# Attention on TensorE: every matmul and transpose issued in source order

## The chip, the cores and the metric

The kernel runs on one core of a Trainium2 chip. The metric is the device time of one execution in microseconds; the number to be predicted is the median of the runs of the changed kernel.

## The reference, cut to what matters

Attention with a position bias, followed by two feed-forward layers. The change is in the attention.

```python
B, H, S, D = 4, 8, 576, 64
scores = q @ k.T / sqrt(D) + bias          # bias: a small network of relative positions, per head
attn = exp(scores - scores.max(-1)) / sum   # row softmax
x = attn @ v                                # then two feed-forward layers on 2304 x 512
```

## The kernel before

Attention is done for 16 units. A unit n is one pair of heads of one batch entry. It has nine steps s: steps 0 to 7 are a block of 128 queries of one head against all 576 keys, and step 8 is the last 64 queries of both heads. A step goes through these stages:

- `scores` (L374): matmuls of the queries with the keys into a PSUM tile `s` (two buffers). Each product is made in two parts, high and low, and two halves of the keys, so a step of 128 queries is four instructions of 288 columns; step 8 has ten.
- VectorE (L378) adds the bias, writes `u` and reduces the row extreme into `stat`; ScalarE (L394) takes the exponential and writes the probabilities `p` (`pm` for step 8) and their row sums.
- `trans` (L432, L437 for step 8): a group of four transposes of 128 x 128 into a PSUM tile `tr`, which one copy moves to `ptm` in SBUF (L424 on VectorE or L422 on ScalarE, by the string PT_EVAC).
- `trans_rem` (L443, and L445 with c = 3): the keys beyond 512, one or two transposes into a tile `tr` of their own, copied to `ptr`.
- `invert` and `turn_inv` (L411): reciprocals of the row sums, spread out and turned by three or two transposes into a tile `tr`, copied to `inv`. The tile of three is copied by ScalarE; the tile of two by VectorE and then a short ScalarE copy.
- `av` (L458, L462): the product with the values into a PSUM tile `av`, and `av_out` (L471), which multiplies by `inv`.

The tiles named `tr`, from `trans`, `trans_rem` and `turn_inv` alike, share three PSUM buffers. A new tile can start only when the copy out of the buffer that it takes has ended.

`slot_of_two(i)` writes out the work of a slot: the scores of its two steps, the AV of older steps (`AV` gives the slots), their exponentials, the reciprocals, the turn of `inv`, and the transposes of the two steps of the slot before. Nine slots, a period, hold two units. Steps of the loading of the feed-forward weights (`load.one_step`, L243 to L255) and a part of the next unit's preparation (`prep`, L346 to L349) are woven in on the other engines.

The source order is not the order of issue. When the program is built, a scheduler lays out a fixed order for every engine by its own plan of the times: an instruction whose inputs or buffer are not ready in the plan lets later ones of its engine pass. On the chip each engine then works through its list in that order. `with tc.issue_after(x)` binds the instructions made inside to come behind x on the same engine. Before, there is one such edge in this part, which keeps the transposes of a slot behind the last score of the slot:

```python
            with tc.issue_after(last_s[0].ins):
                trans(t)
```

Of the kernel before, what the change touches and what calls it, by code (L numbers as in the profile page):

```python
# [1 line left out]

# [1 line left out]

# [14 lines left out]
P = 128  # L19
B, H, S, D = 4, 8, 576, 64  # L20
# [4 lines left out]
HS = S // 2  # L25
# [71 lines left out]
def block_kernel(ctx: ExitStack, tc: tile.TileContext, q, k, v, mlp, w_in, w_out, w_gate, w_val, w_out2, dist_d,  # L97
                 rows_d, out):
    nc = tc.nc
# [199 lines left out]
    Pm = [apool.tile([P, S], F32, name=f"pm{i}") for i in range(2)]  # L299
    ident = apool.tile([P, P], F32, name="ident")  # L300
    stat = apool.tile([P, 5, NSTEP, 2], F32, name="stat")
    low, sums = [stat[:, i, :, 0] for i in range(2)], [stat[:, i, :, 0] for i in range(2, 5)]
    spread = apool.tile([P, 5 * P], F32, name="spread")
# [10 lines left out]
    def load_v(n):  # L314
        vn[n] = a2.tile([P, 10, D], F32, name="vn")
        return nc.sync.dma_start(vn[n], v[n])

    def load_bias(p, c):
        n = min(P, S - P * c)
        rows_of = nbias[c][15 : 15 + n * (8 * RK - 1)].rearrange("(i q) -> i q", i=n)  # L320
        for h in range(2):
            o = bias_t[c][:, h] if c < 4 else bias_m[64 * h : 64 * h + 64]
            i = rows_of[:, RK * (2 * p + h) : RK * (2 * p + h) + S]
            if c == 4 and h == 1:
                nc.sync.dma_start(o[:, 0:512], i[:, 64:S])
                nc.sync.dma_start(o[:, 512:S], i[:, 0:64])
            else:
                nc.sync.dma_start(o, i)
# [23 lines left out]
    NS = NU * NSTEP  # L352
    ptm = apool.tile([P, 2, 4, S], F32, name="ptm")
    ptr = apool.tile([P, S], F32, name="ptr")
    pts, us, avs, last_u, last_s = {}, {}, {}, [None], [None]

    seq = [(n, s) for n in range(NU) for s in range(NSTEP)]

    def keys(s, h, a):

        if s < 8 or h == 0:
            return [(HS * a, 0, HS)]
        return [(64, 0, HS)] if a == 0 else [(64 + HS, 0, HS - 64), (0, HS - 64, 64)]

    def scores(t):
        n, s = seq[t]
        Q, K = Qs[n % 2], Ks[n % 2]
        ps = pp.tile([P, 2, 512], F32, name="s")
        todo = [(s % 2, s // 2)] if s < 8 else [(0, 4), (1, 4)]
        for a in range(2):  # L370
            mm = [(h, c, r, part) for h, c in todo for r in range(2) for part in keys(s, h, a)]
            for i, (h, c, r, (k0, o, w)) in enumerate(mm):
                q0 = (0, S + P)[h] + P * c if c < 4 else (512, S)[h]
                last_s[0] = nc.tensor.matmul(ps[:, a, o : o + w], Q[:, q0 : q0 + P], K[:, r, h, k0 : k0 + w],  # L374
                                             start=(i == 0), stop=(i == len(mm) - 1))
        u = a2.tile([P, S], F32, name="u", bufs=3)
        bt = bias_t[s // 2][:, s % 2] if s < 8 else bias_m
        last_u[0] = nc.vector.tensor_tensor_reduce(  # L378
            out=halves(u), in0=ps[:, :, 0:HS], in1=halves(bt), op0=ALU.add, op1=ALU.min, scale=-0.125, scalar=3e38,
            accum_out=low[n % 2][:, s : s + 1])  # L380
        us[t] = u
# [10 lines left out]
    def expo(t):  # L392
        n, s = seq[t]
        nc.scalar.activation(probs(t), us.pop(t), AF.Exp, bias=low[n % 2][:, s : s + 1], scale=-1.0,  # L394
                             accum_out=sums[n % 3][:, s : s + 1])
# [11 lines left out]
    def turn_inv(n, c0, c1):  # L407

        ps = pp.tile([P, 4, P], F32, name="tr", bufs=3)
        for c in range(c0, c1):  # L410
            nc.tensor.transpose(ps[:, c % 3], spread[:, P * c : P * c + P], ident)  # L411
        if c1 == 3:
            evac("A", inv[:, 0 : 3 * P].rearrange("p (c q) -> p c q", c=3), ps[:, 0:3])
        else:
            evac("V", inv[:, 3 * P : 4 * P], ps[:, 0])
            for h in range(2):
                r = slice(64 * h, 64 * h + 64)
                evac("VA"[h], inv[r, 4 * P : S], ps[r, 1, r])

    def evac(eng, dst, src):  # L420
        if eng == "A":
            nc.scalar.copy(dst, src)  # L422
        else:
            nc.vector.tensor_copy(dst, src)  # L424

    def trans(t):
        n, s = seq[t]
        if s < 8:
            ps = pp.tile([P, 4, P], F32, name="tr", bufs=3)
            c, h = divmod(s, 2)  # L430
            for kc in range(4):
                nc.tensor.transpose(ps[:, kc], pts[n, c][:, h, 64 * h + P * kc : 64 * h + P * kc + P], ident)  # L432
            evac(PT_EVAC[s], ptm[:, h, :, P * c : P * c + P], ps)
        else:
            ps = pp.tile([P, 4, P], F32, name="tr", bufs=3)
            for kc in range(4):
                nc.tensor.transpose(ps[:, kc], Pm[n % 2][:, P * kc : P * kc + P], ident)  # L437
            evac("VA"[n % 2], ptm[:, :, :, 512:S], ps.rearrange("p c (h q) -> p h c q", h=2))

    def trans_rem(n, c):  # L440

        ps = pp.tile([P, 4, P], F32, name="tr", bufs=3)
        nc.tensor.transpose(ps[:, 0], pts[n, c].rearrange("p h s -> p (h s)")[:, 512 : 512 + P], ident)  # L443
        if c == 3:
            nc.tensor.transpose(ps[0:64, 1], Pm[n % 2][:, 512:S], ident)  # L445
            for h in range(2):
                evac("AV"[h], ptr[64 * h : 64 * h + 64, 512:S], ps[0:64, 1, 64 * h : 64 * h + 64])
        evac("A", ptr[:, P * c : P * c + P], ps[:, 0])

    def av(n, a, g):  # L450
        if g == 0:
            avs[a] = pp.tile([P, 512], F32, name="av", bufs=1)
        ps = avs[a]
        vt = vn[n]
        cols = slice(HS * a, HS * a + HS)
        if g < 4:
            for h in range(2):
                nc.tensor.matmul(ps[64 * h : 64 * h + 64, 0:HS], vt[:, 4 * h + g], ptm[:, h, g, cols],  # L458
                                 start=(g == 0), stop=False)
        else:  # L460
            for h in range(2):
                nc.tensor.matmul(ps[64 * h : 64 * h + 64, 0:HS], vt[:, 8 + h], ptr[:, cols], start=False, stop=True)  # L462

    def av_out(n, a):
        p, b = divmod(n, B)
        i = S * b + HS * a
        while i < S * b + HS * a + HS:
            j, o = divmod(i, 2 * TW)
            w = min(2 * TW - o, S * b + HS * a + HS - i)
            k = i - S * b - HS * a  # L470
            nc.vector.tensor_tensor(out=xj[j][:, p, o : o + w], in0=avs[a][:, k : k + w],  # L471
                                    in1=inv[:, HS * a + k : HS * a + k + w], op=ALU.mult)
            i += w

    REM = {1: 0, 3: 1, 5: 2, 8: 3}
# [4 lines left out]
    for n in range(NU):  # L480
        i = (NSTEP * n + 5) // 2 + 2
# [5 lines left out]
    def steps(i):  # L487
        return [t for t in (2 * i, 2 * i + 1) if 0 <= t < NS]

    def slot_of_two(i):  # L490

        for t in steps(i):
            scores(t)
            n, s = seq[t]
            p, b = divmod(n, B)
            if s == 0:
                last_v[0] = load_v(n)
            if b == B - 1 and p + 1 < NPAIR and (s % 2 == 1 or s == 8):
                load_bias(p + 1, s // 2)
        for n, a, g in AV.get(i, ()):  # L500
            av(n, a, g)
            if g == 4:
                av_out(n, a)
        for t in steps(i):
            expo(t)
        for t in steps(i - 1):
            n, s = seq[t]
            if s in (5, 8):
                invert(n, s // 6 * 3, s // 6 * 2 + 3)
        for t in steps(i - 2):  # L510
            n, s = seq[t]
            if s in (5, 8):
                turn_inv(n, s // 6 * 3, s // 6 * 2 + 3)
        for t in steps(i - 1):
            n, s = seq[t]
            with tc.issue_after(last_s[0].ins):
                trans(t)
                if s in REM:
                    trans_rem(n, REM[s])
        for t in steps(i):  # L520
            if t in PREP:
                n, h = PREP[t]
                prep(n, h)
            for k, (n, h) in PREP.items():
                if h == 1 and n + 1 < NU and t == k + 3:
                    load_qk(n + 1)
# [6 lines left out]
    with ExitStack():  # L533
# [15 lines left out]
        ps = bp.tile([P, 2, 512], F32, name="s")[:, 0]  # L549
# [39 lines left out]
        for G in range(NG):  # L589
# [9 lines left out]
            ps = bp.tile([P, 2, 512], F32, name="s")  # L599
            for d0, d1 in ((0, min(nd, 512)), (512, nd)):  # L600
                for ct in range(4):
                    if d0 < d1:
                        nc.tensor.matmul(line(ps)[32 * ct : 32 * ct + 32, d0:d1], w2bd, hid[ct][:, d0:d1],
                                         start=True, stop=True)
# [44 lines left out]
        for i in range(NSLOT):  # L649
            slot_of_two(i)  # L650
            if i == NS // 2:
                w = keep.tile([P, 8 * TW], F32R, name="early")
# [119 lines left out]
        for part2, t in todo:  # L772
            for f in range(NH * part2, NH * part2 + NH):
# [3 lines left out]
                g = begun.pop(f) if f in begun and t == 0 else None  # L777
                if g is None:
                    g = hardswish(fp.tile([P, TW], F32, name="g", bufs=2), project(t, slots[2 * f % NALL]))
# [113 lines left out]
        for v, (p, j) in enumerate(visits):  # L893
# [9 lines left out]
            for n in range(2):  # L903
                t = 2 * j + n
# [48 lines left out]
```

## Time and profile before

| | |
|---|---|
| median of three runs | 1155.64 us (1153.95 to 1157.52) |
| the profiled execution: its time, its span | 1153.65 us, 1151.9 us |
| TensorE busy | 1129.9 us, 98% |
| VectorE busy | 770.0 us, 67% |
| ScalarE busy | 589.0 us, 51% |
| mean granted clock | 1.000 |

The bias is made from 0 to about 57 us, attention runs from there to about 341 us, and the two feed-forward layers fill the rest. PE is TensorE, PEld its weight loads, DVE VectorE, ACT ScalarE. The shares of the whole span average over stages with different limits, so attention is read from stretches of its own.

### The profile page before, as it was taken

The numbers are of one execution on the slowest core, as the hardware profiler recorded it, in microseconds if no ns is written. First come the engines' busy times: TensorE is split into PE (matmuls) and PEld (weight loads), VectorE is DVE, ScalarE is ACT, GpSimd is POOL, SyncE is SP. The second block draws the span as 40 slices with busy tenths as digits, with TensorE's granted clock in tenths as the row PEclk, the third lists the DMA queues.
The fourth block names the chain that finished last, engine by engine and source line by source line (L and its number), as shares of the span: only waits on it lengthen the run. The fifth ranks groups of instructions, "written<-read, shape, count | busy, mean of one in ns | idle before, by whom it ended". The sixth has DMA issues, their size and how long they took to land.

```text
span 1151.9 us, 19179 instructions
## 1 busy us (share of the span) xinstructions
PE 1129.9 (98%) x6878; PEld 1008.9 (88%) x6878; DVE 770.0 (67%) x1487; ACT 589.0 (51%) x1288; POOL 426.2 (37%) x340
## 2 busy tenths in 40 slices
PE   8799999999999999999999999999999999999998
PEld 3287777777789999999999999989899899998997
DVE  8987888897768888365376775585367656643443
ACT  7988888887765544454455454342333232221221
POOL 0154645554225432331347444261333223311311
PEclk9999999999999999999999999999999999999999
DMA  6854546364013665259467659976878848757532
GB/s 206 298 163 121 158 130 177 113 201 116 14 42 110 206 237 187 116 181 340 150 227 276 244 193 366 388 264 251 303 254 311 312 167 316 275 190 247 192 110 74
DMA packets 83503, 236.82 MB, mean 206 GB/s; under 512 B 9936, under 2 KB 12624, under 8 KB 83408
## 3 DMA queue, kind: packets, MB, share of 16 engines
q1 hardware_dynamic: 83408, 235.60, 59.4%
q8 instruction: 54, 0.88, 0.3%
q14 instruction: 41, 0.34, 0.1%
HBM read 154.15 MB, written 81.41 MB: 205 GB/s over the span
## 4 chain that ended last, share of the span: by engine, by line
PE 85%; DVE 5%; ACT 3%; issue 2%; POOL 1%; DMA 1%; DVEq 0%; ACTq 0%; POOLq 0%; SPq 0%
PE o L700 17%; PE h L834 11%; PE o L834 11%; PE o L889 6%; PE h L889 6%; PE h L637 5%; PE h L635 5%; PE h L636 5%; PE s L374 5%; PE av L458 5%; PE tr L432 4%; PE av L462 1%; DVE u L378 1%; PE tr L411 1%; ACT p L394 1%
## 5 line engine op out<-in xcount | busy, mean ns | idle before, releaser
L700 PE MATMUL o<-gh,slot 128*128 128x384 f32 x768 | 195.1, 334 | 1.8 <-DVE take L424 1.8
L700 PEld LDWEIGHTS o<-gh,slot 128*128 128x128 f32 x768 | 138.5, 188 | 2.4 <-DVE take L424 2.1
L700 PE MATMUL o<-gl,slot 128*128 128x384 f32 x384 | 128.5, 335 | 0.7 <-DVE gl L686 0.7
L378 DVE CUSTOM_DVE_ANT_0 u<-s,bias 128x576 f32<-128x576 f32 x128 | 93.7, 754 | 30.3 <-PE s L374 26.8
L374 PE MATMUL s<-k,q 128*128 128x288 f32 (+2 forms) x672 | 111.5, 304 | 1.3 <-DVE stat L378 0.9
L394 ACT ACTIVATE p<-u,stat 128x576 f32<-128x576 f32 x128 | 98.9, 775 | 23.8 <-DVE stat L378 23.3
L870 POOL TENSOR_TENSOR gp<-s,gp 128x384 fp32r<-128x384 f32 x36 | 39.4, 1108 | 176.1 <-ACT gp L869 91.3
L685 ACT CAST gh<-g 128x384 fp32r<-128x384 f32 x94 | 48.5, 516 | 97.3 <-DVE g L642 97.0
L642 DVE SCALAR_TENSOR_TENSOR g<-g,h 128x384 f32<-128x384 f32 x94 | 51.6, 549 | 69.2 <-ACT g L641 69.2
L686 DVE TENSOR_TENSOR gl<-g,gh 128x384 fp32r<-128x384 f32 x94 | 63.3, 673 | 48.2 <-ACT gh L685 47.0
L374 PEld LDWEIGHTS s<-k,q 128*128 128x128 f32 x672 | 92.0, 189 | 2.8 <-issue 1.2
L207 POOL TENSOR_TENSOR hl<-corners,hl 128x512 fp32r<-128x512 f32 x42 | 57.1, 1366 | 94.1 <-ACT hl L206 79.1
L340 POOL TENSOR_TENSOR k<-early,one 128x576 fp32r<-128x576 f32 x30 | 35.0, 1170 | 138.8 <-PE s L374 62.7
L641 ACT ACTIVATE g<-h,half 128x384 f32<-128x384 f32 x94 | 54.5, 580 | 53.1 <-PE h L637 52.6
L458 PE MATMUL av<-ptm,vn 128*64 128x288 f32 x512 | 79.1, 419 | 0.2
L834 PE MATMUL o<-x,slot 128*128 128x384 f32 x432 | 78.2, 336 | 0.0
L834 PE MATMUL h<-x,slot 128*128 128x384 f32 x432 | 77.8, 335 | 0.0
L834 PEld LDWEIGHTS h<-x,slot 128*128 128x128 f32 x432 | 75.2, 188 | 0.7
L834 PEld LDWEIGHTS o<-x,slot 128*128 128x128 f32 x432 | 75.1, 188 | 0.4 <-DVE sum L424 0.3
L432 PE MATMUL tr<-ident,p 128*128 128x128 f32 x512 | 74.0, 277 | 0.4 <-ACT ptr L422 0.2
L700 PEld LDWEIGHTS o<-gl,slot 128*128 128x128 f32 x384 | 72.0, 188 | 1.4 <-DVE gl L686 1.4
L870 POOL TENSOR_TENSOR x<-s,x 128x384 fp32r<-128x384 f32 x36 | 40.9, 1149 | 82.3 <-ACT x L869 48.6
(154 smaller groups left out, 2709.5 us busy)
## 6 DMA issues: line engine op xcount, KB each, us to landing
w<-hl SPq DMA_DIRECT2D x67, 512.0 KB, 3.3
slot<-w SPq DMA_DIRECT2D x67, 512.0 KB, 5.7
raw<-in_part_dram SPq DMA_DIRECT2D x50, 512.0 KB, 4.1
x<-xc SPq DMA_DIRECT2D x56, 384.0 KB, 6.3
sum<-sum SPq DMA_DIRECT2D x72, 256.0 KB, 3.7
early<-xc SPq DMA_DIRECT2D x28, 384.0 KB, 6.0
nbias<-ptm SPq DMA_DIRECT2D x36, 295.5 KB, 3.1
early<-in_part_dram SPq DMA_DIRECT2D x32, 288.0 KB, 4.5
```

The lines of the kernel that those rows point to most:

```text
L374: last_s[0] = nc.tensor.matmul(ps[:, a, o : o + w], Q[:, q0 : q0 + P], K[:, r, h, k0 : k0 + w], start=(i == 0), stop=(i == len(mm) - 1))
L378: last_u[0] = nc.vector.tensor_tensor_reduce(out=halves(u), in0=ps[:, :, 0:HS], in1=halves(bt), op0=ALU.add, op1=ALU.min, scale=-0.125, sc ...
L394: nc.scalar.activation(probs(t), us.pop(t), AF.Exp, bias=low[n % 2][:, s : s + 1], scale=-1.0, accum_out=sums[n % 3][:, s : s + 1])
L432: nc.tensor.transpose(ps[:, kc], pts[n, c][:, h, 64 * h + P * kc : 64 * h + P * kc + P], ident)
L458: nc.tensor.matmul(ps[64 * h : 64 * h + 64, 0:HS], vt[:, 4 * h + g], ptm[:, h, g, cols], start=(g == 0), stop=False)
L635: nc.tensor.matmul(ps[:, 0:TW], wh, XH[:, c], start=(c == 0), stop=False)
L636: nc.tensor.matmul(ps[:, 0:TW], wl, XH[:, c], start=False, stop=False)
L686: last_g[0] = nc.vector.tensor_tensor(out=gl, in0=g, in1=gh.bitcast(F32), op=ALU.subtract)
L700: nc.tensor.matmul(os[c][:, 0:TW], sl[:, r, P * c : P * c + P], x, start=(first and r == 0 and x is gh), stop=(last and x is gl))
L834: nc.tensor.matmul(ps[b], sl[:, r, o : o + P], x[:, c, s], start=(k < 4 and i == 0), stop=(i == len(mm) - 1), skip_group_check=True)
L870: nc.gpsimd.tensor_tensor(out=G[:, i, 1], in0=s, in1=G[:, i, 0].bitcast(F32), op=ALU.subtract)
L889: nc.tensor.matmul(os[i], x[:, P * i : P * i + P], slots[(base + 14 + e) % NALL][:, r], start=first, stop=last)
```

## The change

A context `in_turn` is put around every matmul and transpose of attention. It binds the instruction made inside to the one that the same context made last. With it the scores, the `inv` transposes, the groups, the remainders and AV form one chain on TensorE in source order. The edge to the last score of the slot is dropped, as the chain holds it. The projections of the first feed-forward layer that are begun in the last slots (L657) are not in the chain. The diff without its other places of the same form:

```diff
-    pts, us, avs, last_u, last_s = {}, {}, {}, [None], [None]
+    pts, us, avs, last_u, last_pe = {}, {}, {}, [None], []
+
+    @contextmanager
+    def in_turn():
+        with ExitStack() as order:
+            if last_pe:
+                order.enter_context(tc.issue_after(last_pe[-1].ins))
+            yield last_pe.append
...
-                last_s[0] = nc.tensor.matmul(ps[:, a, o : o + w], Q[:, q0 : q0 + P], K[:, r, h, k0 : k0 + w],
-                                             start=(i == 0), stop=(i == len(mm) - 1))
+                with in_turn() as done:
+                    done(nc.tensor.matmul(ps[:, a, o : o + w], Q[:, q0 : q0 + P], K[:, r, h, k0 : k0 + w],
+                                          start=(i == 0), stop=(i == len(mm) - 1)))
...
-            nc.tensor.transpose(ps[:, c % 3], spread[:, P * c : P * c + P], ident)
+            with in_turn() as done:
+                done(nc.tensor.transpose(ps[:, c % 3], spread[:, P * c : P * c + P], ident))
...
-                nc.tensor.transpose(ps[:, kc], pts[n, c][:, h, 64 * h + P * kc : 64 * h + P * kc + P], ident)
+                with in_turn() as done:
+                    done(nc.tensor.transpose(ps[:, kc], pts[n, c][:, h, 64 * h + P * kc : 64 * h + P * kc + P], ident))
...
-        nc.tensor.transpose(ps[:, 0], pts[n, c].rearrange("p h s -> p (h s)")[:, 512 : 512 + P], ident)
+        with in_turn() as done:
+            done(nc.tensor.transpose(ps[:, 0], pts[n, c].rearrange("p h s -> p (h s)")[:, 512 : 512 + P], ident))
         if c == 3:
-            nc.tensor.transpose(ps[0:64, 1], Pm[n % 2][:, 512:S], ident)
+            with in_turn() as done:
+                done(nc.tensor.transpose(ps[0:64, 1], Pm[n % 2][:, 512:S], ident))
...
-                nc.tensor.matmul(ps[64 * h : 64 * h + 64, 0:HS], vt[:, 4 * h + g], ptm[:, h, g, cols],
-                                 start=(g == 0), stop=False)
+                with in_turn() as done:
+                    done(nc.tensor.matmul(ps[64 * h : 64 * h + 64, 0:HS], vt[:, 4 * h + g], ptm[:, h, g, cols],
+                                          start=(g == 0), stop=False))
...
-            with tc.issue_after(last_s[0].ins):
-                trans(t)
-                if s in REM:
-                    trans_rem(n, REM[s])
+            trans(t)
+            if s in REM:
+                trans_rem(n, REM[s])
```

## Rows read from the trace of the kernel before

**Rows 1.** The page: busy us (share of span) x count; a group's busy us, mean ns

```profile
PE 1129.9 (98%) x6878; PEld 1008.9 (88%) x6878; DVE 770.0 (67%) x1487; ACT 589.0 (51%) x1288; POOL 426.2 (37%) x340
...
L432 PE MATMUL tr<-ident,p 128*128 128x128 f32 x512 | 74.0, 277 | 0.4 <-ACT ptr L422 0.2
```

**Rows 2.** Stretches: length, busy us of each engine, granted clock, DMA share, GB/s

```profile
99.40:133.70 34.30, 34.19 (x259) 26.17 (x259) 28.93 (x73) 28.82 (x74) 18.57 (x14) 1.00 0.61 181
...
271.20:306.30 35.10, 33.78 (x257) 25.78 (x256) 24.94 (x69) 27.64 (x73) 16.08 (x12) 1.00 0.17 45
```

**Rows 3.** TensorE's waits, whole span: total us, times, longest us

```profile
PE tr L443 <- ACT inv L422: 1.8, 4, 0.7
PE o L700 <- DVE take L424: 1.8, 1, 1.8
...
PE s L374 <- DVE stat L378: 0.9, 4, 0.3
```

**Rows 4.** Timeline, TensorE, a whole run: start us, length us, what

```profile
210.08 1.31 PE L374 MATMUL s<-k,q 128*128 128x288 f32 x8
211.33 0.95 PE L458 MATMUL av<-ptm,vn 128*64 128x288 f32 x6
```

**Rows 5.** Timeline, TensorE, place 1 in unit 9

```profile
213.21 0.60 PE L432 MATMUL tr<-ident,p 128*128 128x128 f32 x4
213.65 0.27 PE L443 MATMUL tr<-ident,p 128*128 128x128 f32 x1
213.67 0.90 PE L374 MATMUL s<-k,q 128*128 128x288 f32 x5
214.49 0.65 PE L432 MATMUL tr<-ident,p 128*128 128x128 f32 x4
214.90 0.64 PE L374 MATMUL s<-k,q 128*128 128x288 f32 x3
215.47 0.46 PE L458 MATMUL av<-ptm,vn 128*64 128x288 f32 x2
```

**Rows 6.** Timeline, TensorE, place 1, the first and the last of eight

```profile
77.09 0.90 PE L374 MATMUL s<-k,q 128*128 128x288 f32 x5
...
317.83 0.90 PE L374 MATMUL s<-k,q 128*128 128x288 f32 x5
```

**Rows 7.** Timeline, ScalarE, place 1 in unit 9

```profile
212.86 0.77 ACT L394 ACTIVATE p<-u,stat 128x576 f32<-128x576 f32 x1
...
213.84 0.59 ACT L422 COPY ptm<-tr 128x512 f32<-128x512 f32 x1
```

**Rows 8.** Timeline, TensorE, place 2 of unit 2

```profile
89.06 0.33 PE L443 MATMUL tr<-ident,p 128*128 128x128 f32 x1 [0.45 <-ACT inv L422]
...
89.25 0.64 PE L374 MATMUL s<-k,q 128*128 128x288 f32 x3
89.82 0.71 PE L458 MATMUL av<-ptm,vn 128*64 128x288 f32 x4
```

**Rows 9.** Timeline, places 2 and 3 of unit 10, TensorE and then ScalarE

```profile
224.95 0.60 PE L437 MATMUL tr<-ident,pm 128*128 128x128 f32 x4
...
226.76 0.71 PE L458 MATMUL av<-ptm,vn 128*64 128x288 f32 x4
...
229.79 0.90 PE L374 MATMUL s<-k,q 128*128 128x288 f32 x5
230.62 0.71 PE L458 MATMUL av<-ptm,vn 128*64 128x288 f32 x4
...
225.08 0.47 ACT L422 COPY inv<-tr 128x384 f32<-128x384 f32 x1
...
229.44 0.21 ACT L422 COPY inv<-tr 64x64 f32<-64x64 f32 x1
```

**Rows 10.** Timeline, TensorE, place 3 of unit 14

```profile
299.79 0.51 PE L374 MATMUL s<-k,q 128*128 128x288 f32 x2
300.23 0.46 PE L458 MATMUL av<-ptm,vn 128*64 128x288 f32 x2
```

More of the change, by code (lines that the diff above doesn't have):

```diff
@@ L1 @@
-from contextlib import ExitStack
+from contextlib import ExitStack, contextmanager
 import numpy as np
@@ L436, in trans @@
             for kc in range(4):
-                nc.tensor.transpose(ps[:, kc], Pm[n % 2][:, P * kc : P * kc + P], ident)
+                with in_turn() as done:
+                    done(nc.tensor.transpose(ps[:, kc], Pm[n % 2][:, P * kc : P * kc + P], ident))
             evac("VA"[n % 2], ptm[:, :, :, 512:S], ps.rearrange("p c (h q) -> p h c q", h=2))
@@ L457, in av @@
             for h in range(2):
-                nc.tensor.matmul(ps[64 * h : 64 * h + 64, 0:HS], vt[:, 4 * h + g], ptm[:, h, g, cols],
-                                 start=(g == 0), stop=False)
+                with in_turn() as done:
+                    done(nc.tensor.matmul(ps[64 * h : 64 * h + 64, 0:HS], vt[:, 4 * h + g], ptm[:, h, g, cols],
+                                          start=(g == 0), stop=False))
         else:
             for h in range(2):
-                nc.tensor.matmul(ps[64 * h : 64 * h + 64, 0:HS], vt[:, 8 + h], ptr[:, cols], start=False, stop=True)
+                with in_turn() as done:
+                    done(nc.tensor.matmul(ps[64 * h : 64 * h + 64, 0:HS], vt[:, 8 + h], ptr[:, cols], start=False,
+                                          stop=True))
     def av_out(n, a):
```

## The prediction

> **What bounds the kernel now.** I read the profile from the outside in. The page's first part shows TensorE busy 98% of the span [rows 1]. Cut into stretches, a period of attention (two units, about 34.3 us, eight of them between 65 and 341 us) has TensorE busy for all but 0.1 to 1.3 us at a granted clock of 1.00, while ScalarE and VectorE have 5 us or more free [rows 2]. So in attention the sum of TensorE's intervals sets the end: a microsecond added there is added to the kernel, unless a later wait gives it back. TensorE's waits inside attention are few; the largest is a remainder transpose (L443) that waits for ScalarE's copy of `inv`, 1.8 us in four places [rows 3].
>
> A matmul record is longer than its share of the array, so I price by distances from start to start. An undisturbed run of eight score matmuls takes 1.25 us to the start of the AV matmul behind it (210.08 to 211.33) [rows 4]; four transposes inside a run of transposes take 0.44 us (213.21 to 213.65) [rows 5].
>
> **What the change can reorder.** AV, the `inv` transposes and the scores already stand in source order in the timelines that I looked at. What stands out of order is scores of the next slot, ahead of transposes of this one. A period has three such places, where the timeline shows a run of eight scores cut in two:
> Place 1: after two `inv` transposes, a group of four and a remainder, five scores are issued, then the next group of four, then the other three scores [rows 5]. It comes 8 times with the same counts (the last at 317.83) [rows 6].
> Place 2: after three `inv` transposes and two groups, scores (four or five; once one) stand ahead of the two remainder transposes. 7 times [rows 8, 9].
> Place 3, in the slot behind place 2: scores stand ahead of the second group, of the remainder, or of both. 7 times [rows 9, 10].
> All three are slots with four tiles named `tr`, and the pool has three buffers. The change takes the cut away and puts those scores behind the fourth tile. No instruction is added, no DMA is issued or moved, and no queue but TensorE's own is passed.
>
> **The gain.** At place 1 the cut stretch takes 1.80 us, from 213.67 to 215.47 [rows 5]. Whole it would be 0.44 + 1.25 = 1.69, so a cut costs about 0.11 us. With 8 + 7 + some 10 cuts (place 3 often has two) their removal is worth 25 x 0.11 = 2.8 us, if the fourth tile never waits.
>
> **The loss.** It does wait. At place 1 the second group starts at 214.49, and ScalarE's copy of the first group out of its buffer (`ptm`, L422) ends at 213.84 + 0.59 = 214.43 [rows 7]: the group starts 0.06 us behind it. The copy comes so late because it stands behind the slot's second exponential (212.86 to 213.63) [rows 7]. The five scores were filling that wait. In strict order the remainder starts at 213.65 and the group could follow at 213.76, but its buffer is free only for 214.49, so TensorE stands still for 0.73 us. All eight scores then start where the last three do now, at 214.90 [rows 5], and AV follows 1.25 later at 216.15 in place of 215.47: 0.68 us later, net of the saved cut. Eight times: 5.4 us. Behind the waiting group stands everything on TensorE; for its scores VectorE's reduction (L378) waits, and for that ScalarE's exponential, so neither can run ahead and win the time back.
>
> Place 2, two of the seven read off. Unit 10: the remainder could start at 224.95 + 0.44 = 225.39; the `inv` copy ends at 225.08 + 0.47 = 225.55, so it starts near 225.61, scores 0.19 later (as 89.06 to 89.25 [rows 8]) at 225.80, and AV at 227.05 in place of 226.76 [rows 9]: 0.29. Unit 2: the remainder waits until 89.06 already now; the eight scores would start at 89.25 and AV at 90.50 in place of 89.82 [rows 8]: 0.68. Few of these remainders wait today [rows 3], so I take six like unit 10 and one like unit 2: 2.4 us.
>
> Place 3. Unit 10: the remainder waits for the `inv` copy, which ends at 229.44 + 0.21 = 229.65, and scores start behind it at 229.79; with eight in place of five AV starts at 231.04, not 230.62 [rows 9]: 0.42. Unit 14: 299.79 + 1.25 = 301.04 in place of 300.23 [rows 10]: 0.81. Six like the first and one like the second are 3.3 us, if the copies stay where they are in relation to TensorE. But place 2 has just pushed TensorE back by 0.3, and ScalarE has room [rows 2], so the copy need not move back as far. The price lies between nothing and 3.3; having no row that is nearer to either end, I take half, 1.7 us.
>
> **Sum.** 5.4 + 2.4 + 1.7 = 9.5 us. Waits elsewhere may give some back: the scores' waits for VectorE (0.9 us) and the one wait of L700 for `take` (1.8 us) [rows 3] end on engines that gain time while TensorE stands. I take off a third of these 2.7, 0.9, which leaves 8.6. The profiled execution's own time is 1153.65 us (its span of 1151.9 and 1.75 around it), so 1162.3 for it. The median of the runs, 1155.64, is 2.0 above it, so the forecast for the median is 1164.2.
>
> **Rivals.**
> *A, the copies come in another order (16%).* If ScalarE's short `inv` copy (0.21, as in [rows 9]) goes ahead of the `ptm` copy right behind the exponential, and the fourth tile takes its buffer, the group at place 1 starts near 214.15: 0.34 lost in place of 0.68, 2.7 us in all. With half of place 2, none of place 3 and the same 0.9 given back that is +3.0: 1158.6. For it: both copies are of tiles that TensorE ends within half a microsecond, so a small shift can swap them. Against it: `ptm` goes first now [rows 7], and nothing on TensorE up to there changes.
> *B, faster (11%).* One mechanism: with TensorE's order fixed, the copies that free the fourth tile's buffer are laid ahead of the second exponential, and the tile never waits. Then the cuts' 2.8 us and the 1.8 us of waits for `inv` are saved: 1151.0. It decides from the point at which the copy ends 0.7 us earlier than 214.43. Against it: the first group ends on TensorE only at 213.21 + 0.60 = 213.81, with that exponential long begun, so a copy of 0.59 can't be in time; only `inv`'s buffer could.
> *C, the waits spread (9%).* Scores that start later put the exponentials later, and slots with three tiles begin to wait too. One further wait of 0.37 in each of 16 units is +5.9: 1170.1. Against it: the groups of four sat idle for 0.4 us in all [rows 1], and ScalarE has 5 us free in a period [rows 2].
> *D, the clock (2%).* The granted clock is 1.00, its level of 2.4 GHz, in each stretch of attention, transposes included [rows 2]. By that row whole runs change nothing and the sum stands. If transposes in longer runs brought it to 1.2 GHz, the 512 of L432 [rows 1], now 0.11 us apart, would take 0.11 more each: +56 us, 1212. The Trainium skill, "TensorE: Matmul & The Clock Gate", section "Part 4: PE-mode transpose", says that transposes do not count as busy for the clock as matmuls do; by that rule whole runs of them speak against the change. The trace so far does not bear it out.
> *E, the order stays (4%)*: if the scores keep their place ahead of the waiting tile, 1155.6. Against it: the diff ties each TensorE instruction of attention to the one before it.
>
> **The numbers.** My forecast has 58% and a range of its own from 1159.5 (place 1 at two thirds, half of place 2, none of place 3) to 1169.5 (all of place 2 like unit 2, place 3 in full, nothing given back). About 0.3%, 3.5 us, is what a measurement of this kernel can tell from no change. Slower by more: the 58, 7 of A's 16, C and D, 76%. Within: 9 of A, and E, 13%. Faster: B, 11%. The range for eight in ten runs from 1155 to 1171: it leaves out B, D and the far part of C.
>
> **What would show it.** At place 1 of the new timeline: an unbroken run of eight scores, 1.25 us to AV, and ahead of it a second group that starts 0.06 us behind a ScalarE copy. Among the waits: transposes into `tr` waiting for ScalarE's copies for some 8 x 0.7 + 7 x 0.3 = 7.7 us or more, in place of 1.8 to 2.0. A period longer by about 1.1 us. Stretches behind attention that keep their length to a microsecond. I am wrong if the copies end before the fourth tile comes to the head of the queue, or if what lies behind 341 us shrinks by as much as attention grows.

## The result and the profile after

The changed kernel takes 1164.22 us (median of four runs, 1163.14 to 1165.24) against 1154.8 us for the kernel before, now with four runs. The ratio is 1.0084 with a 95% interval from 1.0064 to 1.0104: slower by 9.4 us between the medians and 9.7 by the ratio. The profiled execution has a span of 1161.4 us where it was 1151.9, 9.5 us more.

The stretches show where. One period of the kernel after and its stretch from the last AV matmul to the end (length, busy us of PE, PEld, DVE, ACT and POOL, granted clock, DMA share, GB/s):

```profile
171.60:207.40 35.80, 34.53 (x259) 26.03 (x257) 28.72 (x73) 28.57 (x73) 18.60 (x14) 1.00 0.58 173
...
346.40:1161.40 815.00, 808.18 (x4444) 778.82 (x4440) 498.05 (x782) 311.61 (x614) 288.18 (x233) 1.00 0.64 231
```

The same last stretch of the kernel before:

```profile
336.30:1151.90 815.60, 808.64 (x4444) 778.77 (x4440) 498.89 (x782) 312.64 (x614) 289.71 (x233) 1.00 0.65 230
```

This period is 1.5 us longer than the first one in [rows 2], and TensorE's idle part has grown from 0.1 us to 1.3. What lies behind attention is 0.6 us shorter, not longer. The clock is 1.00 in both stretches.

TensorE's waits in the kernel after (total us, times, longest), to be held against [rows 3]:

```profile
PE tr L443 <- ACT ptm L432: 4.7, 8, 0.8
PE tr L456 <- ACT inv L432: 3.8, 8, 1.1
...
PE o L716 <- DVE take L434: 1.8, 1, 1.8
...
PE s L383 <- DVE stat L387: 1.1, 3, 0.4
PE tr L443 <- ACT ptr L432: 0.9, 1, 0.9
PE s L383 <- DVE stat L410: 0.7, 1, 0.7
```

The first row is new: eight waits of a group of four transposes for ScalarE's `ptm` copy. The second was 1.8 us in four places and is 3.8 in eight. The scores' waits for VectorE's `stat`, 0.9 us before, are 1.1 + 0.7 = 1.8 now.

Place 1 of the kernel after in unit 7, TensorE's timeline, against [rows 5]:

```profile
182.86 0.60 PE L443 MATMUL tr<-ident,p 128*128 128x128 f32 x4
183.29 0.27 PE L456 MATMUL tr<-ident,p 128*128 128x128 f32 x1
184.13 0.65 PE L443 MATMUL tr<-ident,p 128*128 128x128 f32 x4 [0.57 <-ACT ptm L432]
184.54 1.29 PE L383 MATMUL s<-k,q 128*128 128x288 f32 x8
185.76 0.46 PE L473 MATMUL av<-ptm,vn 128*64 128x288 f32 x2
```

and ScalarE's at the same time, against [rows 7]:

```profile
182.50 0.76 ACT L403 ACTIVATE p<-u,stat 128x576 f32<-128x576 f32 x1
...
183.49 0.58 ACT L432 COPY ptm<-tr 128x512 f32<-128x512 f32 x1
184.10 0.21 ACT L432 COPY inv<-tr 64x64 f32<-64x64 f32 x1
```

The remainder starts at 183.29 and the next group not 0.11 but 0.84 us later, 0.06 behind the end of the copy (183.49 + 0.58 = 184.07). The scores are one run of eight, 1.22 us from their start to AV. ScalarE's order is as it was: exponential, `ptm`, `inv`.

Places 2 and 3 in unit 6, first TensorE and then ScalarE, against [rows 9]:

```profile
159.62 0.60 PE L449 MATMUL tr<-ident,pm 128*128 128x128 f32 x4
160.27 0.33 PE L456 MATMUL tr<-ident,p 128*128 128x128 f32 x1
...
160.46 1.29 PE L383 MATMUL s<-k,q 128*128 128x288 f32 x8
161.69 0.71 PE L473 MATMUL av<-ptm,vn 128*64 128x288 f32 x4
...
163.08 1.04 PE L443 MATMUL tr<-ident,p 128*128 128x128 f32 x8
164.40 0.33 PE L456 MATMUL tr<-ident,p 128*128 128x128 f32 x1 [0.28 <-ACT inv L432]
164.48 1.30 PE L383 MATMUL s<-k,q 128*128 128x288 f32 x8
165.71 0.46 PE L473 MATMUL av<-ptm,vn 128*64 128x288 f32 x2
```

```profile
159.75 0.47 ACT L432 COPY inv<-tr 128x384 f32<-128x384 f32 x1
...
164.14 0.21 ACT L432 COPY inv<-tr 64x64 f32<-64x64 f32 x1
```

The remainder at 160.27 stands 0.65 us behind the start of the group ahead of it, where 0.44 is undisturbed, and starts 0.05 after the `inv` copy ends (159.75 + 0.47 = 160.22). The one at 164.40 starts 0.05 after the short `inv` copy ends (164.35), where the eight transposes ahead of it ran out near 163.96 (163.08 + 8 x 0.11).

To add this up I matched the 64 AV runs of the two traces and took, for each, its start after less its start before; what this shift gains from one AV run to the next belongs to the work between them. Sums over attention: ahead of the first AV -0.56 us; at place 1 +5.21 (eight times 0.65); in the slots between place 1 and place 2 +0.70; at place 2 +2.10; at place 3 +2.64; at the other AV runs nothing beyond 0.03 in all. That is 10.1 us, less the 0.6 behind attention 9.5, the growth of the span.

The +0.70 between places 1 and 2 is the sum of jumps of +0.5 in units 4, 8 and 12 and of -0.45 in units 6 and 10. Each jump is one wait that came, went or grew: in the slot ahead of place 2 the fifth of the eight scores waits for VectorE to be done with `stat` (the reduction; in unit 12 the list names the reciprocals, L410). Before, it waited so in units 6, 10 and 12, for 0.16 to 0.21 us; now it does in units 4, 8 and 12, for 0.36, 0.38 and 0.70. The one ahead of place 2 in unit 8 of the kernel after:

```profile
191.72 0.77 PE L383 MATMUL s<-k,q 128*128 128x288 f32 x4 [0.38 <-DVE stat L387]
```

### The profile page after: what moved, and what is told of

The parts are those of the page before. It is cut to its first block, busy times and chain, and to the rows that moved or that the text cites. A ratio compares the mean times of both kernels' runs of the same rounds, so it can differ in the third digit from the quotient of the medians.

```text
span 1161.4 us, 19174 instructions
## 1 busy us (share of the span) xinstructions
PE 1130.9 (97%) x6878; PEld 1008.7 (87%) x6878; DVE 766.8 (66%) x1487; ACT 586.4 (50%) x1288; POOL 424.3 (37%) x340
## 4 chain that ended last, share of the span: by engine, by line
PE 71%; DVE 2%; POOL 1%; issue 1%; ACT 1%; DMA 1%; POOLq 0%; ACTq 0%; SPq 0%
PE o L716 17%; PE h L850 11%; PE o L850 10%; PE o L905 6%; PE h L905 6%; PE h L652 5%; PE h L653 5%; PE h L651 5%; PE s L383 2%; PE av L473 1%; PE tr L443 1%; DVE z L188 0%; POOL hl L207 0%; POOL gp L886 0%; DVE z L190 0%
## 5 line engine op out<-in xcount | busy, mean ns | idle before, releaser
L383 PE MATMUL s<-k,q 128*128 128x288 f32 (+2 forms) x672 | 105.4, 301 | 2.2 <-DVE stat L387 1.1
L657 ACT ACTIVATE g<-h,half 128x384 f32<-128x384 f32 x94 | 54.3, 577 | 52.3 <-PE h L653 51.7
L443 PEld LDWEIGHTS tr<-ident,p 128*128 128x128 f32 x512 | 57.0, 141 | 17.8 <-issue 7.0
```

The costliest lines, as they stand in the source:

```text
L383: done(nc.tensor.matmul(ps[:, a, o : o + w], Q[:, q0 : q0 + P], K[:, r, h, k0 : k0 + w], start=(i == 0), stop=(i == len(mm) - 1)))
L443: done(nc.tensor.transpose(ps[:, kc], pts[n, c][:, h, 64 * h + P * kc : 64 * h + P * kc + P], ident))
```

## The experiments

The theory is that of the prediction: a slot's fourth tile `tr` waits for one of three buffers, and scores that were free to pass it used to fill the wait. The rival is that source order itself costs, by switches or by the other engines' orders, which are laid out anew around the chain. All runs are compared with the kernel before on the same chip; the changed kernel stands at 1.0084. A ratio difference of 0.001 is 1.15 us. The intervals of the changed kernel (0.0020 to either side) and of an experiment (0.0013) make about 2.7 us to either side of the gain of one over the other, so in the first three experiments the times alone don't tell the theory from its rival; the traces must.

**Place 1 set free.** The last group at place 1 is still bound to come behind the remainder, but nothing is bound to come behind it:

```diff
+    @contextmanager
+    def let_pass():
+        with tc.issue_after(last_pe[-1].ins):
+            yield lambda made: None
...
+            hold = let_pass if (n % 2, s) == (1, 2) else in_turn
             for kc in range(4):
-                with in_turn() as done:
+                with hold() as done:
```

> The chain stays on everything but the last group of four at place 1 (odd units, step 2): that group may be passed by scores. Theory (the fourth tr tile of a slot waits for its buffer, and scores used to fill the wait): the cut comes back at the 8 places 1 only, TensorE's 8 waits of 0.73 us for the ptm copy go, and the kernel gains 8 x 0.65 = 5.2 us on the changed kernel, about 1159. Rival (the loss comes from the other engines' orders, laid out anew around the chain, and not from these waits): the chain is nearly whole here, so at most 1 or 2 us come back.

Measured 1159.62 us, ratio 1.0052 (1.0040 to 1.0065): 3.7 us regained by the ratios. The eight waits for `ptm` are gone from TensorE's list; its largest wait in attention, and its timeline at place 1:

```profile
PE tr L463 <- ACT inv L438: 4.9, 9, 1.2
```

```profile
181.96 0.90 PE L389 MATMUL s<-k,q 128*128 128x288 f32 x5
182.77 0.66 PE L450 MATMUL tr<-ident,p 128*128 128x128 f32 x4
183.18 0.64 PE L389 MATMUL s<-k,q 128*128 128x288 f32 x3
183.75 0.71 PE L480 MATMUL av<-ptm,vn 128*64 128x288 f32 x4
```

Five scores, group, three scores have come back; from the first score to AV it is 1.79 us. The shift of the AV runs against the changed kernel falls by 0.65 at each of the eight places, 5.21 in all, as the theory has it. The execution doesn't show all of it: the start of attention (0.73) and the slots from place 1 to place 3 (0.8 together, with longer waits for `inv`) took more time, which leaves 3.65, and behind attention 2.0 us were lost, of which the granted clock explains 1.5. Stretches of this run (columns as above), and the matmul that ended a wait:

```profile
384.00:386.00 2.00, 1.04 (x5) 1.05 (x6) 1.89 (x5) 1.53 (x4) 0.00 (x0) 0.94 0.43 102
386.00:388.00 2.00, 2.00 (x7) 2.00 (x7) 2.00 (x4) 0.92 (x2) 1.33 (x1) 0.50 0.97 381
388.00:390.00 2.00, 2.00 (x10) 2.00 (x10) 1.55 (x3) 0.39 (x1) 0.00 (x0) 0.71 0.97 389
```

```profile
384.96 0.62 PE L723 MATMUL o<-gh,slot 128*128 128x384 f32 x2 [1.76 <-DVE take L440]
```

TensorE stood 1.76 us for `take`, as in [rows 3], and soon after ran at 0.50, the 1.2 GHz level, for 3.4 us. The hundredth matmul behind the wait starts 1.5 us later, counted from the wait's end, than in the changed kernel, where the same wait of 1.77 us left the clock at 1.00. The profiled executions of the next two experiments show the same dip, so their spans are 1.5 us long for a reason that isn't theirs.

**Places 2 and 3 set free**, by the same edit on the remainder with c = 3 of odd units, the second group of even ones and their first remainder.

> The chain stays on everything but the remainder transposes at place 2 and the second group and the remainder at place 3. Theory: waits at places 2 and 3 go back to those of the kernel before, places 1 keep 0.73 us each; gain on the changed kernel 2.1 + 2.6 + about 0.7 = 4.7 to 5.4 us, about 1159, and together with the run that frees place 1 the two gains add up to the whole loss of 9 to 10 us. Rival: 1 or 2 us, and the two do not add up.

Measured 1160.56 us, ratio 1.0059 (1.0047 to 1.0072): 2.9 us regained. TensorE's waits in attention:

```profile
PE tr L450 <- ACT ptm L438: 4.8, 8, 0.8
PE tr L464 <- ACT inv L438: 1.5, 3, 0.7
```

The eight waits for `ptm` are all still there; those for `inv` are back at 1.5 us. The shift falls by 2.47 at places 2 and by 2.34 at places 3. In the traces the two experiments give 5.21 + 4.81 = 10.0 us at the freed places, as much as attention grew. Not all of it reaches the end of attention: over all AV runs the two traces gain 3.65 and 4.22, 7.9 together; the start of attention took 0.73 and 0.38 back, the slots between the places the rest. The 0.7 that was expected from the slots ahead of place 2 did not come back (they were 0.2 longer). By the ratios it is 3.7 + 2.9 = 6.6 of 9.7, less than expected; with these intervals the times alone neither prove nor refute the sum.

**The buffer freed earlier.** The chain is whole; the short second `inv` copy moves from ScalarE, where two exponentials stand ahead of it, to VectorE:

```diff
-                evac("VA"[h], inv[r, 4 * P : S], ps[r, 1, r])
+                evac("V", inv[r, 4 * P : S], ps[r, 1, r])
```

> The whole chain, and the short second copy of the two-transpose inv tile goes to VectorE behind VectorE's first one, so this tile's buffer comes free without ScalarE, which has two exponentials in front. Theory: the fourth tile takes that buffer some 0.35 us earlier at places 1 and 3: 8 x 0.35 + 7 x 0.35 = 5 us gained on the changed kernel, about 1159 to 1160, unless the layout still hands the fourth tile the ptm buffer at place 1 (then place 3 alone, 2 us). Rival (order of other engines, not buffers): no gain beyond 1 us.

Measured 1161.65 us, ratio 1.0065 (1.0052 to 1.0077): 2.2 us regained, half of what was expected. Place 1, TensorE's timeline:

```profile
181.99 0.27 PE L456 MATMUL tr<-ident,p 128*128 128x128 f32 x1
182.58 0.63 PE L443 MATMUL tr<-ident,p 128*128 128x128 f32 x4 [0.32 <-DVE inv L434]
182.96 1.29 PE L383 MATMUL s<-k,q 128*128 128x288 f32 x8
```

The group now waits for VectorE's `inv` copy, 0.59 us behind the start of the remainder where it was 0.84. The gain is 0.16 to 0.30 at each place 1, 2.1 in all, and 2.1 at places 3 (0.95 of it in unit 14). VectorE's copy ends at 182.43, 0.44 behind the start of the remainder, where ScalarE's `ptm` copy ended 0.78 behind it. A wait named after another copy, which ends 0.34 earlier, and 0.25 shorter, speaks for the buffer; why the group starts 0.15 behind this copy and not 0.06 stays open. In its trace attention is 4.2 us shorter; 1.5 of it is lost to the clock dip.

**No fourth tile.** The chain is whole, and the remainder transpose of such a slot goes into free columns of the `inv` tile, ahead of that tile's copies; the 64-row remainder of odd units moves into the next `inv` tile, one slot on. All the work is done.

```diff
+        guest = (n, 3) if c1 == 3 and n % 2 else (n + 1, 0) if c1 == 5 and n + 1 < NU else None
+        if guest:
+            with in_turn() as done:
+                done(nc.tensor.transpose(ps[:, c1 % 3 if c1 == 5 else 3], pts[guest].rearrange("p h s -> p (h s)")[:, 512 : 512 + P], ident))
+        if c1 == 5 and n % 2:
+            with in_turn() as done:
+                done(nc.tensor.transpose(ps[0:64, 3], Pm[n % 2][:, 512:S], ident))
...
+        if guest:
+            seen.add(guest)             # trans_rem skips it
+            evac("A", ptr[:, P * guest[1] : P * guest[1] + P], ps[:, c1 % 3 if c1 == 5 else 3])
```

> The whole chain, but the remainder transpose that makes the fourth tile shares the inv tile (its free columns), so that every slot has at most three tr tiles; the 64-row remainder of odd units moves one slot later into the same kind of tile. Nothing is left out. Theory: no tile waits for a buffer, whole runs then cost nothing and save the cuts: 8 x 0.11 at place 1, and the waits for inv that the kernel before still had at places 2 and 3: 1155 - 0.9 - 2 - 2 = about 1150, faster than both kernels. Rival (source order itself is what costs, through switches or other engines): it stays at 1162 to 1165.

Measured 1148.77 us, ratio 0.9960 (0.9947 to 0.9974): 1.2% faster than the changed kernel and 0.4% faster than the one before, with the chain on. TensorE's largest waits from 57 to 347 us, and its timeline at a place 1:

```profile
PE o L733 <- DVE gl L719: 0.7, 1, 0.7
PE s L383 <- DVE stat L387: 0.5, 2, 0.3
```

```profile
211.25 0.44 PE L423 MATMUL tr<-ident,spread 128*128 128x128 f32 x2
211.52 0.27 PE L427 MATMUL tr<-ident,p 128*128 128x128 f32 x1
211.63 1.04 PE L458 MATMUL tr<-ident,p 128*128 128x128 f32 x8
212.43 1.30 PE L383 MATMUL s<-k,q 128*128 128x288 f32 x8
213.66 0.71 PE L490 MATMUL av<-ptm,vn 128*64 128x288 f32 x4
```

No transpose waits for a copy any more, and the whole slot runs through: two `inv` transposes, the remainder, eight transposes, eight scores, AV. So source order by itself isn't what costs, and the rival falls. Built without the chain, the shared-tile kernel has the same order on all five engines; where no tile has to wait the scheduler makes whole runs of its own accord.

**A cut by itself.** In the shared-tile kernel the second group at place 1 is put behind the fifth score by hand:

```diff
-            trans(t)
+            if (n % 2, s) != (1, 2):
+                trans(t)
...
+                if (n % 2, s, a, i) == (1, 6, 0, 0):   # in scores, behind the matmul
+                    trans(t - 4)
```

> The shared-tile kernel, in which no tr tile waits, with one cut put back by hand at each of the 8 places 1: the second group of four stands behind the fifth score of the next slot. It measures a cut by itself. Theory: 0.11 to 0.13 us each, from scores to AV 1.80 us for eight scores and a group in place of 1.69, about 1 us on the shared-tile kernel (1148.8), 1149.8. If whole runs themselves are worth more than I think, it is slower by 3 us or more.

Measured 1148.67 us, ratio 0.9951 (0.9937 to 0.9965), within the noise the same as without the cuts; an effect of 1 us would not show in these times, but it would in the trace. TensorE's timeline:

```profile
211.57 0.27 PE L429 MATMUL tr<-ident,p 128*128 128x128 f32 x1
211.68 0.60 PE L460 MATMUL tr<-ident,p 128*128 128x128 f32 x4
212.04 0.91 PE L383 MATMUL s<-k,q 128*128 128x288 f32 x5
212.78 0.60 PE L460 MATMUL tr<-ident,p 128*128 128x128 f32 x4
213.14 0.64 PE L383 MATMUL s<-k,q 128*128 128x288 f32 x3
213.71 0.71 PE L492 MATMUL av<-ptm,vn 128*64 128x288 f32 x4
```

From the remainder to AV it is 213.71 - 211.57 = 2.14 us, and without the cut 213.66 - 211.52 = 2.14. At all eight places the time between the AV runs around the cut is the same to 0.01 us. A cut between scores and transposes costs nothing.

**Two buffers in place of three**, with and without the chain (`bufs=2` for the four tiles `tr`).

> The changed kernel with two tr buffers in place of three, to double the suspected cost. Theory: now the third tile of every slot waits, some 0.4 to 0.8 us in each of 72 slots, with no score to fill the time: 30 to 50 us slower than the changed kernel, 1195 to 1215. Rival (buffers have little to do with it): within 5 us.

> The kernel before with two tr buffers. Theory: scores pass the waiting tiles as they did at places 1 to 3, now in every slot, so it loses much less than the chained kernel does with two buffers: 10 to 20 us over the kernel before, 1165 to 1175. If the order has no part in it, it loses as much as the chained one does.

Measured 1215.01 us with the chain, ratio 1.0519 (1.0499 to 1.0539), at the upper end of what was expected, and 1173.67 us without, ratio 1.0161 (1.0147 to 1.0176), within it. TensorE's waits with the chain, and then without it:

```profile
PE tr L443 <- ACT ptm L432: 18.1, 16, 2.6
PE tr L456 <- ACT ptm L432: 8.1, 12, 0.7
PE tr L456 <- DVE ptm L434: 5.4, 12, 0.8
```

```profile
PE s L374 <- DVE stat L378: 2.0, 4, 0.7
...
PE tr L411 <- ACT ptm L422: 1.3, 1, 1.3
```

With two buffers the chain costs 1.0519 - 1.0161 = 0.0358 of the time before, 41 us; with three it cost 0.0084, 9.7 us; where no slot has more tiles than buffers, nothing, as the order is the same with and without it. With the chain and two buffers TensorE's transposes wait 68 times in attention, 47.5 us in all, near the 72 waits that were expected. An estimate: at most 5 of the 41 us are the granted clock, as that trace has three stretches of 3.4 us in attention at 0.50, and the one without the chain none. Without the chain the listed waits are few, yet attention is 15.9 us longer than with three buffers. There the AV runs are cut up too (79 in place of 64); whether these cuts cost it, or waits too short for the list, no run separates.

## Why the prediction was right, point by point

*TensorE's intervals set the end.* Right: 10.1 us more in attention, 0.6 less behind it.

*Place 1, 0.68 us eight times.* Measured 0.65 each, 5.2 in place of 5.4; the difference is the run of eight scores, 1.22 us to AV where 1.25 was put in. The mechanism is shown: the wait is named in the trace, it goes when the order is loosened at that place, shrinks when the buffer is freed earlier, and goes when there is no fourth tile.

*Place 2, 2.4 us.* Measured 2.1, but against the kernel before the seven shifts are 0.63, 0.05, 0.56, 0.05, 0.57, 0.14 and 0.10 (units 2 to 14), none near the 0.29 that was taken for six of them: the jumps in the slot ahead move them, and that they cancel to 2.1 is luck. Counted with those jumps it is 2.8. The run with places 2 and 3 set free, which keeps the jumps, shows the price itself: 0.66, 0.28, 0.25, 0.27, 0.28, 0.61 and 0.12, 2.47 in all. The pricing held (unit 12 stands above it and unit 14 below).

*Place 3, half of 3.3, 1.7 us.* Mis-sized: measured 2.6. The halving rested on the thought that ScalarE's copy would not move back as far as TensorE does at place 2. It did, nearly: counted from the start of the AV run at place 2, the short `inv` copy ends 0.23 us earlier to 0.13 later than before, 0.6 earlier in the sum of the seven, and 3.3 less 0.6 is 2.7. Why it moves along is argued, not tested: the exponentials ahead of it wait for these same delayed scores.

*Waits elsewhere give back 0.9.* Wrong in its mechanism. Neither wait that was named gave anything back: that for `take` is 1.8 us before and after, and the scores' waits for VectorE grew from 0.9 to 1.8 us, and from them come the 0.7 lost between places 1 and 2, which were not foreseen. What was given back is 0.56 at attention's start and 0.6 behind it, 1.2 in all. The chain doesn't account for the start: with place 1 set free, where the chain is the same up to there, the first AV run stands 0.17 later than in the kernel before. So that the size is near is luck; where the 1.2 come from stays open.

*A cut costs 0.11 us, and their removal is worth 2.8.* Wrong. The hand-made cut costs nothing. What I took for the price of a cut was the tail of the wait itself: at place 1 the group began 0.06 us behind the copy even with five scores in front, so those scores didn't cover it quite. It did no harm to the sum, since both the stretch with the cut and the one without were read off as they stood, but rival B's 2.8 us for cuts had nothing in it. The shared-tile kernel won its 0.4% by removing waits: in its trace attention is 5.2 us shorter than before, and 0.13 of it at each place 1 (once 0.34) is that tail.

*The other rivals.* The copies kept their order (A), they came no earlier (B), three-tile slots did not begin to wait (C: the AV runs behind them shift by at most 0.03 us in all), the order did change (E). The clock stayed at 1.00 with whole runs of transposes (D), and in the shared-tile kernel with the run of eleven shown above (1.000 over its whole profiled execution). The Trainium skill's rule of "TensorE: Matmul & The Clock Gate", section "Part 4: PE-mode transpose", that transposes do not count as busy in the way that matmuls do, had no effect here that a trace shows.

The signs that were named came: ScalarE's copies hold up transposes for 4.7 + 3.8 = 8.5 us where 7.7 or more was expected, what lies behind attention kept its length to 0.6 us, and the seven periods that hold all three places grew by 0.9 to 1.6 us, 1.4 in the mean, where 1.1 was expected. The upper end of the forecast's own range comes by its terms to 1169.2, not 1169.5; nothing hangs on it.

That the median came out at the predicted figure is partly luck. The forecast was +8.6 on 1155.64; measured is +9.5 in the span and +9.4 on a median that a fourth run moved to 1154.8. Place 3 and the 0.7 us were short by 1.6 together, places 1 and 2 long by 0.5, and what was given back was 0.3 more than assumed.

## What to carry to other kernels

Where a list of instructions looks out of order, look for the wait that the stray instructions fill, before putting them back: on an in-order engine a strict order turns each hidden wait into a stall (0.65 us at each place 1). Count the tiles that one slot takes from a pool against the pool's buffers; a slot with one tile too many waits for a copy of the same slot, with its whole chain of reduction and exponential in front. The remedy here was to take the tile away by sharing free columns, and then the order took care of itself.

## What the runs showed of the hardware that was not expected

Alternating between score matmuls and transposes costs TensorE nothing: 2.14 us for a remainder, eight transposes and eight scores, cut or not. This holds for these two alone, not for cuts in AV.

A wait for `take` of 1.76 or 1.77 us, which the kernels before and after have too, was followed in four profiled executions (the first three experiments, and two buffers without the chain) by 3.4 us at the 1.2 GHz level, and in four (before, after, shared tile, cut by hand) by none. It costs 1.5 us, so two executions can differ by that much with no difference in their waits. What decides it stays open.
